# Weight conversion shared with GpSimd, a copy in halves, and a new order in the first turn of a gated linear attention + SSM kernel

## The chip, the cores and the metric

The kernel runs on one core of a Trainium2 chip. The metric is device time in microseconds (us), the median of several runs. All arithmetic is in float32, except the handling of the weights' bits. The engines are TensorE (PE, with its weight loads PEld), VectorE (DVE), ScalarE (ACT), GpSimd (POOL) and SyncE (SP, which here only issues DMAs).

## The reference

Two blocks follow each other: a gated linear recurrence over 4 batches x 8 heads x 768 steps with head dimension 48, and a gated state space block with model width 384 and inner width 512. `w_in`, `A_log` and `w_out` come as float64.

```python
for t in range(S):
    state = alpha[:, :, t, :, None] * state + np.einsum('bhd,bhe->bhde', k[:, :, t], v[:, :, t])
    y[:, :, t] = np.einsum('bhd,bhde->bhe', q[:, :, t], state)
x = y.transpose(0, 2, 1, 3).reshape(B, S, H * D)
proj = x @ w_in
val, gate = (proj[..., :D_inner], proj[..., D_inner:])
a = np.exp(A_log)[None, None, :]
for t in range(S):
    h = a[0, 0] * h + val[:, t, :]
    ys[:, t, :] = h
silu = gate * (1.0 / (1.0 + np.exp(-gate)))
out = silu * ys @ w_out
```

## The kernel before

The 4 x 768 steps are cut into 12 groups of 256 steps. A group `m` is prepared (attention inputs), then attended, then projected and written out; in turn `n` the projection and output of group `n` run beside the attention of group `m = n + 1` and the preparation of group `n + 2`. There is no scheduler: each engine runs its instructions in the order in which the source issues them, and the tile framework only adds the waits that data and buffers need.

**Preparation.** `alpha`, `q` and `k` arrive with time on the partitions. Groups 0 to 2 are turned by PE against an identity matrix: `turned` (L663) issues 16 matmuls (each runs as two passes, so the profile counts 32) into a pair of PSUM banks, and ACT copies the pair into SBUF: `alphas` (L677) for alpha, `straighten` (L681) for q and k. Later groups are turned by DVE (`products`, L643). Then DVE makes two running products along time, `P` (`scan_P`, L616) and `V` (`scan_V`, L625), and scales k by V and q by P (`scaled_k`, L600, into `Zk`; `scaled_q`, L593, into `Zq`).

**Attention of a group.** `first` multiplies `Zk` with `Zq` on PE (`scores`, L695) and masks the result (`masks`, L708: DVE one half, ACT a copy of the other, POOL its mask, L722). `second` forms half of the values and the states (`values`, `states`), which ACT copies into `dS` and POOL adds up (`add_up`, L785). `third` adds what the sums carry (`carried`), the other half of the values, and brings the result into the layout of the projection, `xT` (`join`, L843), by ACT copies and small DMAs ("moves"). In turn 0 half of the moves are issued by POOL, half by SP. Group 0 has shorter functions of its own (`first_values`, `first_states`, `first_carried`, `first_join`).

**Projection and output.** `project(n, cc)` (L858) handles a quarter of the inner width: six matmuls write the value half and the gate half of the PSUM tile `pvg`; DVE scans the first half into `hh`, ACT takes the silu of the second into `sg`; the returned function makes POOL multiply them into `f`. `output(n)` (L877) multiplies the four quarters of `f` by `w_out`. Its tile `pair` has two banks, one for each 128 steps: the first three quarters for both, then the last quarter for both, then ACT copies the two halves to `o_sb` and SP sends them off.

**Weights.** [...] `low(i)` (L531) is an ACT copy that scales the low words into an int32 tile `wr` (two buffers); `convert(i)` (L537) is a DVE shift (L544), a DVE OR (L546) and an int32 add of `wr` (L548, which the profile shows as `CUSTOM_DVE_ANT_0`). 128 x 768 words a piece. Projection `cc` needs piece `cc`, output pieces 4 and 5.

**Start.** `wide` holds v of group 0 with zeros between the heads, so that one matmul can cover a window; `wide_S` likewise for the first states. POOL clears all of `wide` (L892) and then issues the loads of v into it, builds the identity (`make_identity`), fills the ends of the raw tiles (L510), and copies the identity into `Zq` (L514). DVE clears `ends` and the rest in `constants` (L490). `keep_warm` (L686) issues three matmuls on zeros ahead of the first real work, from `ends`.

**Order of turn 0 before** (calls in the source; each puts its instructions at the end of their engines' queues):

```python
f0 = project(n, 0); low(2); tq = straighten(1, "q"); f0(); V = scan_V(1, P)
f1 = project(n, 1); low(3); scaled_k(1, tk, V); scaled_q(1, tq, P); alphas(2)
tk = straighten(2, "k"); convert(2); first(m); low(4); tq = straighten(2, "q"); f1()
convert(3); f2 = project(n, 2); second(m); low(5); f2(); convert(4)
f3 = project(n, 3); third(m); f3(); convert(5); P = scan_P(2); V = scan_V(2, P)
scaled_k(2, tk, V); scaled_q(2, tq, P)
```

(`load_...` and `junk` calls are left out here; `junk` is an ACT check of alpha that nothing waits for.)

Of the kernel before, what the change touches and what calls it, by code (L numbers as in the profile page):

```python
# [9 lines left out]
FP32 = mybir.dt.float32  # L10
# [3 lines left out]
ALU = mybir.AluOpType  # L14
# [331 lines left out]
def fast(  # L346
# [64 lines left out]
    def steps_of(name, m):  # L411
        return raws[name][:, ds(m % 2 * (2 * ROW + 16), 2 * ROW + 16)]
# [14 lines left out]
    def load_v(m, engine):  # L427
        if m >= N:
            return
        b, g = divmod(m, NG)  # L430
        for c in range(G):
            if m:
                to = vs[m % NV][:, c, :, 0:D]
            else:
                to = wide[:, c].rearrange("p (h d) -> p h d", d=D)[:, ::2, :]
            engine.dma_start(out=to, in_=v[b, :, ds(g * GC + c * C, C), :].rearrange("h p d -> p h d"))
# [51 lines left out]
    flag = const.tile([1, 1], I32, name="flag")  # L488

    def constants():  # L490
        nc.vector.memset(ends, 0.0)
        for al in als:
            nc.vector.memset(al[:, ::GP], 0.0)
        nc.vector.memset(minus, -1.0)
        nc.vector.memset(one, 1.0)
        nc.vector.memset(lower, FLOOR)
        for t in wide_S:
            nc.vector.memset(t, 0.0)
        nc.scalar.activation(spare, minus, AF.Exp)
        for t in vs:  # L500
            nc.vector.memset(t[:, :, :, D:64], 0.0)
        for t in dS[0] + dS[1]:
            nc.vector.memset(t[:, :, :, D:64], 0.0)
        for t in sums:
            nc.vector.memset(t[:, :, D:64], 0.0)
        nc.vector.memset(K0[:, :, :, D:], 0.0)
        make_identity(nc, ident)
        for name in "aqk":
            for m in range(2):
                nc.gpsimd.memset(steps_of(name, m)[:, 2 * ROW:], 1.0)  # L510
        for n, t in enumerate(Zqs):
            for i in range(2):
                rows = ds(64 * i, 64)
                nc.gpsimd.tensor_copy(out=t[rows, :, :, 0:D].rearrange("p u h d -> p (u h) d"),  # L514
                                      in_=ident[rows, None, ds(64 * i, D)].to_broadcast([64, 8 * G, D]))
            if n == 0:
                nc.gpsimd.memset(tri, 1.0)
                nc.gpsimd.affine_select(out=tri, in_=tri, compare_op=ALU.is_ge, fill=0.0, base=0,
                                        channel_multiplier=-1, pattern=[[1, C]])
                for h in range(2):  # L520
                    nc.gpsimd.tensor_copy(out=mask[ds(L * h, L)], in_=tri[ds(L * h, L), ds(L * h, L)])
# [15 lines left out]
    def convert(i):  # L537
        if i not in lows:
            low(i)
        bits, w = bits_of(i)  # L540
        hi = bits[:, :, :, 1]
        t = w.bitcast(U32)
        r = lows.pop(i)
        nc.vector.tensor_scalar(out=t, in0=hi, scalar1=3, scalar2=0x3FFFFFFF,  # L544
                                op0=ALU.logical_shift_left, op1=ALU.bitwise_and)
        nc.vector.scalar_tensor_tensor(out=t, in0=hi, scalar=0xC0000000, in1=t,  # L546
                                       op0=ALU.bitwise_and, op1=ALU.bitwise_or)
        nc.vector.tensor_tensor(out=w.bitcast(I32), in0=w.bitcast(I32), in1=r, op=ALU.add)  # L548

    def check_w(i):  # L550
        hi = bits_of(i)[0][:, :, :, 1].bitcast(FP32)
# [27 lines left out]
    def by_place(t):  # L579
        return t[:, 0:4 * GP].rearrange("p (h t) -> p h t", h=4)  # L580

    def by_runs(t):
        return t.rearrange("p h (c j) -> p h c j", j=NJ)
# [76 lines left out]
        yield  # L660


    def turned(m, name, t):  # L663
        raw = steps_of(name, m)
        tp = t.rearrange("p b x -> p (b x)").rearrange("p (j x) -> p j x", j=NJ)
        for j in range(NJ):
            for i in range(2):
                nc.tensor.matmul(tp[ds(64 * i, 64), j], raw[:, ds(i * ROW + j * D, 64)], ident,  # L668
                                 start=True, stop=True, skip_group_check=True)
        return tp.rearrange("p j (c h) -> p h c j", h=4)  # L670

    def bank_pair(tag=None):
        if tag:
            return ps_at.tile([C, 2, 512], FP32, tag=tag, name=tag)
        return ps_mm.tile([C, 2, 512], FP32, tag="mm", name="mm")

    def alphas(m, tag=None):  # L677
        nc.scalar.activation(by_runs(by_place(als[m % 2])[:, :, 1:GP]),  # L678
                             turned(m, "a", bank_pair(tag)), AF.Copy)

    def straighten(m, name, tag=None):  # L681
        t = plain(name)
# [3 lines left out]
    def keep_warm(n, w, tag="y"):  # L686
        t = bank_pair(tag)[:, 0]
        for _ in range(n):
            nc.tensor.matmul(t[:, 0:w], ends.rearrange("p h t -> p (h t)")[:, 0:C], ends.rearrange("p h t -> p (h t)")[:, 0:w], start=True, stop=True, skip_group_check=True)


    NS = S // L
# [184 lines left out]
    def output(n):  # L877
        b, g = divmod(n, NG)
        pair = ps_mm.tile([C, 2, 512], FP32, tag="mm", name="o")
        os = [pair[:, c, 0:DM] for c in range(G)]  # L880
        for ccs in (range(NI - 1), range(NI - 1, NI)):
            for c in range(G):
                for cc in ccs:
                    nc.tensor.matmul(os[c], fs[n][:, cc, ds(c * C, C)], w_outs[cc // 2][:, cc % 2, :],  # L884
                                     start=(cc == 0), stop=(cc == NI - 1))
        for c in range(G):
            o_sb = p2.tile([C, DM], FP32, tag="o_sb", name="o_sb")
            nc.scalar.activation(o_sb, os[c], AF.Copy)  # L888
            nc.sync.dma_start(out=out[b, ds(g * GC + c * C, C), :], in_=o_sb)


    nc.gpsimd.memset(wide, 0.0)  # L892
    both = [nc.sync, nc.scalar]
    load_steps("a", 0, both)
    load_steps("q", 0, both)
    load_steps("k", 0, both)
    load_steps("a", 1, [nc.sync])
    load_v(0, nc.gpsimd)
    for name in "kq":
        load_steps(name, 1, [nc.sync])  # L900
    nc.scalar.dma_start(out=a_log, in_=moe_A_log.rearrange("(a p) -> p a", p=C))
# [9 lines left out]
            next(steps, None)  # L911

    keep_warm(3, 256)
    alphas(0, "s")
    tq = straighten(0, "q")
    tk = straighten(0, "k")
    load_steps("a", 2, [nc.sync])
# [12 lines left out]
    tk = straighten(1, "k")  # L930
    scores(0)
    masks(0, True)
    P = scan_P(1)
    first_values(True)
    first_states(states(0))
    low(0)
    convert(0)
    first_carried((1,))
    first_values(False)
    first_carried((2, 3))  # L940
    first_join()
    for half in range(2):
        load_w_out(half, nc.sync)
    load_v(2, nc.sync)
    low(1)
    convert(1)
    junk(0)

    def first(m):
# [18 lines left out]
    for n in range(N):  # L968
        m = n + 1
        if n == 0:  # L970
            f0 = project(n, 0)
            low(2)
            tq = straighten(1, "q")
            f0()
            V = scan_V(1, P)
            f1 = project(n, 1)
            low(3)
            scaled_k(1, tk, V)
            scaled_q(1, tq, P)
            alphas(2)  # L980
            load_raw("a", 3, nc.sync)
            tk = straighten(2, "k")
            load_raw("k", 3, nc.sync)
            convert(2)
            first(m)
            low(4)
            tq = straighten(2, "q")
            f1()
            convert(3)
            f2 = project(n, 2)  # L990
            second(m)
            low(5)
            f2()
            convert(4)
            f3 = project(n, 3)
            third(m)
            load_v(3, nc.sync)
            load_raw("q", 3, nc.sync)
            f3()
            convert(5)  # L1000
            junk(1)
            P = scan_P(2)
            V = scan_V(2, P)
            scaled_k(2, tk, V)
            scaled_q(2, tq, P)
            junk(2)
        else:
            first(m)
            if n > 1:
                load_raw("q", n + 2, nc.sync)  # L1010
            go(1)
            f0 = project(n, 0)
            second(m)
            f0()
            load_raw("a", n + 3, nc.sync)
            go(2)
            f1 = project(n, 1)
            f1()
            if n == N - 2:
                for i in range(0, 2):  # L1020
                    check_w(i)
            third(m)
            load_v(m + 2, nc.sync)
            load_raw("k", n + 3, nc.sync)
            go(1)
            f2 = project(n, 2)
            f2()
            if n == N - 2:
                check_w(2)
            if n == N - 1:  # L1030
                check_flag()
            go(1)
            f3 = project(n, 3)
            f3()
            go(2)
        if n == N - 2:
            for i in range(3, NW):
                check_w(i)
            check_end()
        if n == N - 1:  # L1040
            value = nc.values_load(flag[0:1, 0:1], min_val=0, max_val=1)
        output(n)
# [39 lines left out]
```

## Time and profile before

| | us |
|---|---|
| median of 3 runs (lowest to highest) | 293.84 (293.11 to 293.91) |
| profiled execution | 296.36 |
| its span (first to last instruction) | 294.6 |
| PE busy | 278.6 (95%) |
| DVE busy | 215.3 (73%) |
| POOL busy | 112.0 (38%) |
| ACT busy | 108.0 (37%) |
| mean granted PE clock | 0.982 |
| start of the first projection (group 0, quarter 0) | 25.38 |
| start of turn 1 (scores of group 2) | 59.10 |

The profile is of one execution, with some us of its own. Instructions are named by engine, line, output and inputs. The "chain of waits" follows back from the last instruction to what released it; in order of time it shows which engine led when. The timeline lists instructions with start and duration, and in brackets how long the engine was idle before and what ended that. The table by stretches of time gives each engine's busy time (and instruction count), then the granted clock of PE (1.00 is full), the DMA share and GB/s. A line of waits names who waited, for whom, the total, the number of times and the longest. An engine that is off the chain costs nothing by being idle.

### The profile page before, as it was taken

To read this page: it belongs to the slowest core of one execution; us is meant where nothing else is said; L and a number is where in the kernel's file an instruction comes from. 1 tells how busy PE (TensorE), PEld (TensorE's weight loads), DVE (VectorE), ACT (ScalarE), POOL (GpSimd) and SP (SyncE) were. 2 spreads that over 40 slices of the span, in tenths; PEclk is the share of its full clock that TensorE was granted. 3 is DMA by queue.
4 is the path that set the end of the run, shared out by engine and by line. 5 is a ranking of instruction groups with operands and counts; after the bars stand their busy time and mean duration, and the time that the engine had idled before them with its cause. 6 is when DMAs were issued, how large, how long until landed. Compare 5 with 4: busy or idle time off the path is not lost.

```text
span 294.6 us, 9484 instructions
## 1 busy us (share of the span) xinstructions
PE 278.6 (95%) x4064; PEld 220.8 (75%) x4064; DVE 215.3 (73%) x254; ACT 108.0 (37%) x235; POOL 112.0 (38%) x126
## 2 busy tenths in 40 slices
PE   7979999599999999999999999999999999999990
PEld 5967886288778788688688688787787786886860
DVE  6798888939859768689597697697698697269320
ACT  2565556323335244144135235325333351421111
POOL 8300346315416417237146056155155173141110
PEclk9999999959999999999999999999999999999997
DMA  6999580813396494693691891981973911100101
GB/s 203 351 265 365 136 174 17 194 57 89 74 246 141 108 260 92 155 233 65 152 271 41 179 242 51 226 185 47 253 154 86 248 30 32 57 17 25 56 6 61
DMA packets 51812, 41.57 MB, mean 141 GB/s; under 512 B 27344, under 2 KB 49552, under 8 KB 51760
## 3 DMA queue, kind: packets, MB, share of 16 engines
q1 hardware_dynamic: 50544, 39.72, 52.6%
q8 instruction: 34, 0.56, 0.8%
q10 hardware_dynamic: 960, 0.59, 0.8%
q0 software_dynamic: 256, 0.56, 0.6%
q14 instruction: 18, 0.15, 0.2%
HBM read 32.88 MB, written 4.72 MB: 128 GB/s over the span
## 4 chain that ended last, share of the span: by engine, by line
PE 86%; DVE 8%; issue 1%; ACT 1%; POOL 1%; DVEq 0%; POOLq 0%
PE pvg L866 45%; PE o L884 19%; PE y L738 4%; PE s L765 4%; PE y L751 4%; PE s L704 3%; PE mm L704 3%; DVE P L621 2%; DVE V L638 2%; DVE Zk L605 1%; DVE Zq L596 1%; PE s L668 1%; PE y L813 1%; PE y L805 1%; PE mm L668 1%
## 5 line engine op out<-in xcount | busy, mean ns | idle before, releaser
L866 PE MATMUL pvg<-xT,w_in 128*128 128x256 f32 x576 | 135.6, 389 | 0.6 <-ACT xT L827 0.6
L866 PEld LDWEIGHTS pvg<-xT,w_in 128*128 128x128 f32 x576 | 107.6, 192 | 18.1 <-ACT xT L827 0.7
L875 POOL TENSOR_TENSOR f<-sg,hh 128x256 f32<-128x256 f32 x48 | 57.2, 1193 | 68.4 <-ACT sg L874 68.4
L884 PE MATMUL o<-w_out,f 128*128 128x384 f32 x192 | 64.5, 487 | 1.1 <-DVE w_out L548 0.7
L874 ACT ACTIVATE sg<-pvg 128x256 f32<-128x256 f32 x48 | 18.4, 384 | 101.4 <-DVE hh L869 72.6
L884 PEld LDWEIGHTS o<-w_out,f 128*128 128x128 f32 x192 | 36.2, 190 | 24.6 <-issue 1.3
L869 DVE TENSOR_TENSOR_SCAN hh<-a_dec,hh,pvg 128x256 f32<-128x256 f32 x32 | 23.5, 733 | 25.8 <-PE pvg L866 25.0
L722 POOL TENSOR_TENSOR AK<-AK,mask 128x512 f32<-128x512 f32 x11 | 14.6, 1328 | 69.8 <-ACT AK L720 69.8
L785 POOL TENSOR_TENSOR sum<-sum,dS 128x192 f32<-128x192 f32 x37 | 27.4, 739 | 24.1 <-ACT dS L773 22.4
L621 DVE TENSOR_TENSOR_SCAN P<-al,lower 128x1028 f32<-128x1028 f32 x12 | 27.8, 2313 | 3.6 <-ACT al L678 3.4
L638 DVE TENSOR_TENSOR_SCAN V<-al,ends 128x1028 f32<-128x1028 f32 x12 | 27.9, 2322 | 0.1
L888 ACT ACTIVATE o_sb<-o 128x384 f32<-128x384 f32 x24 | 10.5, 488 | 45.4 <-PE o L884 41.5
L719 DVE TENSOR_TENSOR A<-s,mask 128x256 f32<-128x256 f32 x11 | 4.7, 424 | 21.2 <-PE s L704 21.2
L586 DVE STREAM_TRANSPOSE al<-raw_a 128x1024 f32<-128x1024 f32 x9 | 18.4, 2045 | 0.0
L586 DVE STREAM_TRANSPOSE k<-raw_k 128x1024 f32<-128x1024 f32 x9 | 18.4, 2042 | 0.0
L586 DVE STREAM_TRANSPOSE q<-raw_q 128x1024 f32<-128x1024 f32 x9 | 18.2, 2019 | 0.0
L704 PEld LDWEIGHTS s<-Zq,Zk 48*64 48x64 f32 x384 | 10.1, 140 | 9.9 <-issue 9.9
L869 DVE TENSOR_TENSOR_SCAN hh<-a_dec,pvg 128x256 f32<-128x256 f32 x16 | 10.8, 675 | 9.1 <-PE pvg L866 9.1
L704 PE MATMUL s<-Zq,Zk 48*64 48x112 f32 x384 | 12.7, 273 | 4.0 <-DVE Zq L596 4.0
L751 PEld LDWEIGHTS y<-Zq,sum 48*64 48x64 f32 x656 | 12.0, 134 | 4.5 <-POOL sum L785 2.7
L751 PE MATMUL y<-Zq,sum 48*64 48x64 f32 x656 | 14.7, 222 | 0.6 <-issue 0.6
L596 DVE TENSOR_TENSOR Zq<-q,P 128x1024 f32<-128x1024 f32 (+1 forms) x13 | 14.8, 1141 | 0.3
(121 smaller groups left out, 344.3 us busy)
## 6 DMA issues: line engine op xcount, KB each, us to landing
out_dram<-o_sb SPq DMA_DIRECT2D x24, 192.0 KB, 3.6
v<-in_v_dram SPq DMA_DIRECT2D x22, 192.0 KB, 3.7
raw_a<-in_alpha_dram SPq DMA_DIRECT2D x18, 184.0 KB, 4.8
raw_k<-in_k_dram SPq DMA_DIRECT2D x18, 184.0 KB, 4.4
raw_q<-in_q_dram SPq DMA_DIRECT2D x18, 184.0 KB, 4.0
raw_a<-in_alpha_dram SPq DMA_DIRECT2D x18, 176.0 KB, 5.1
raw_k<-in_k_dram SPq DMA_DIRECT2D x18, 176.0 KB, 4.4
raw_q<-in_q_dram SPq DMA_DIRECT2D x18, 176.0 KB, 4.2
```

Source lines behind the costliest of these rows:

```text
L586: nc.vector.transpose(out=by_runs(to).rearrange("p h c j -> p h j c"), in_=raws[name][:, 0:4 * ROW].rearrange("p (h j d) -> p h j d", h=4, ...
L596: nc.vector.tensor_mul(Zqs[m % 2][:, ds(u0, n), :, D:].rearrange("p u h t -> p h u t"), t[:, :, at].rearrange("p h (u t) -> p h u t", t=L) ...
L621: nc.vector.tensor_tensor_scan(out=P, data0=al[:, 0:4 * GP], data1=lower.rearrange("p h t -> p (h t)"), initial=0.0, op0=ALU.mult, op1=ALU ...
L638: nc.vector.tensor_tensor_scan(out=V[:, ::-1], data0=al[:, 1:4 * GP + 1][:, ::-1], data1=ends.rearrange("p h t -> p (h t)")[:, ::-1], init ...
L704: nc.tensor.matmul(scs[m][c][ds(L * h, L), i, ds(p * (L + D), L + D)], Zk[rows, c, p, ds(h * L, L)], Zq[rows, u, p], start=True, stop=True ...
L751: nc.tensor.matmul(ys[m][ds(64 * s, 64), i, e, ds(u * L, L)], Ss[j][rows, p, :], Zqs[m % 2][rows, u, p, D:], start=False, stop=True, skip_ ...
L785: nc.gpsimd.tensor_add(Ss[j][:, :, 0:D], Ss[j - 1][:, :, 0:D], part)
L866: nc.tensor.matmul(pj, w_ins[cc][:, kk, vg, :], xT[:, kk, :], start=(kk == 0), stop=(kk == NK - 1))
L869: nc.vector.tensor_tensor_scan(out=hh, data0=a_dec[:, cc:cc + 1].to_broadcast([C, GC]), data1=pv, initial=prev_h[cc][:, GC - 1:GC] if n % ...
L874: nc.scalar.activation(sg, pg, AF.Silu)
L875: return lambda: nc.gpsimd.tensor_mul(fs[n][:, cc, :], sg, hh)
L884: nc.tensor.matmul(os[c], fs[n][:, cc, ds(c * C, C)], w_outs[cc // 2][:, cc % 2, :], start=(cc == 0), stop=(cc == NI - 1))
```

## The change

1. **Start.** The identity is built first on POOL, then its copies into the first `Zq`, and only then are the loads of v issued. The ends of the raw tiles and the zeros of `wide` are set by DVE, of `wide` and `wide_S[1:]` the gaps alone. `wide_S[0]` is cleared first, and `keep_warm` reads it.
2. **First alpha.** PE turns the first half, ACT copies it, PE turns the second half, ACT copies it.
3. **Weights.** The int32 add of `convert` is issued on POOL.
4. **Before turn 0.** `convert(0)` and `convert(1)` come earlier, the scan P of group 1 after them; q of group 1 is straightened and its scan V made before turn 0.
5. **Turn 0.** Each `f` product follows its projection directly; conversions 3 and 4 and P of group 2 come before projection 2, conversion 5 before projection 3, V of group 2 and the last product `f3` before the attention's third part with its moves.
6. **Output.** In every turn the copy and the DMA of the first half are issued after its last matmul, ahead of the last matmul of the second half.

```diff
     def constants():
-        nc.vector.memset(ends, 0.0)
+        make_identity(nc, ident)
+        nc.vector.memset(wide_S[0], 0.0)
+        for name in "aqk":
+            for m in range(2):
+                nc.vector.memset(steps_of(name, m)[:, 2 * ROW:], 1.0)
+        for c in range(G):
+            nc.vector.memset(wide[:, c].rearrange("p (h d) -> p h d", d=D)[:, 1::2, :], 0.0)
...
+        nc.vector.memset(ends, 0.0)
+        for t in wide_S[1:]:
+            nc.vector.memset(t.rearrange("p (h d) -> p h d", d=D)[:, 1::2, :], 0.0)
...
             if n == 0:
+                load_v(0, nc.gpsimd)
                 nc.gpsimd.memset(tri, 1.0)
...
-        nc.vector.tensor_tensor(out=w.bitcast(I32), in0=w.bitcast(I32), in1=r, op=ALU.add)
+        nc.gpsimd.tensor_tensor(out=w.bitcast(I32), in0=w.bitcast(I32), in1=r, op=ALU.add)
...
-    def alphas(m, tag=None):
-        nc.scalar.activation(by_runs(by_place(als[m % 2])[:, :, 1:GP]),
-                             turned(m, "a", bank_pair(tag)), AF.Copy)
+    def alphas(m, tag=None, parts=1):
+        t = bank_pair(tag)
+        to = by_runs(by_place(als[m % 2])[:, :, 1:GP])
+        for n in range(parts):
+            js = range(NJ // parts * n, NJ // parts * (n + 1))
+            tp = turned(m, "a", t, js)
+            nc.scalar.activation(to[:, :, :, js.start:js.stop], tp[:, :, :, js.start:js.stop], AF.Copy)
...
-            nc.tensor.matmul(t[:, 0:w], ends.rearrange("p h t -> p (h t)")[:, 0:C], ends.rearrange("p h t -> p (h t)")[:, 0:w], start=True, stop=True, skip_group_check=True)
+            nc.tensor.matmul(t[:, 0:w], wide_S[0][:, 0:C], wide_S[0][:, 0:w], start=True, stop=True,
+                             skip_group_check=True)
...
+        def evict(c):
+            o_sb = p2.tile([C, DM], FP32, tag="o_sb", name="o_sb")
+            nc.scalar.activation(o_sb, os[c], AF.Copy)
+            nc.sync.dma_start(out=out[b, ds(g * GC + c * C, C), :], in_=o_sb)
+
         for ccs in (range(NI - 1), range(NI - 1, NI)):
             for c in range(G):
                 for cc in ccs:
                     nc.tensor.matmul(os[c], fs[n][:, cc, ds(c * C, C)], w_outs[cc // 2][:, cc % 2, :],
                                      start=(cc == 0), stop=(cc == NI - 1))
-        for c in range(G):
-            o_sb = p2.tile([C, DM], FP32, tag="o_sb", name="o_sb")
-            nc.scalar.activation(o_sb, os[c], AF.Copy)
-            nc.sync.dma_start(out=out[b, ds(g * GC + c * C, C), :], in_=o_sb)
...
+                if ccs.stop == NI:
+                    evict(c)
...
-    nc.gpsimd.memset(wide, 0.0)
...
-    load_v(0, nc.gpsimd)
...
-    alphas(0, "s")
+    alphas(0, "s", 2)
...
-    P = scan_P(1)
+    low(0)
+    convert(0)
     first_values(True)
     first_states(states(0))
-    low(0)
-    convert(0)
+    low(1)
+    convert(1)
+    P = scan_P(1)
     first_carried((1,))
     first_values(False)
     first_carried((2, 3))
     first_join()
+    tq = straighten(1, "q")
+    V = scan_V(1, P)
...
-    low(1)
-    convert(1)
```

The order of turn 0 after the change, written as above:

```python
f0 = project(n, 0); low(2); scaled_k(1, tk, V); f0(); f1 = project(n, 1)
scaled_q(1, tq, P); alphas(2); f1(); tk = straighten(2, "k"); convert(2); low(3); first(m)
convert(3); tq = straighten(2, "q"); low(4); convert(4); P = scan_P(2)
f2 = project(n, 2); f2(); second(m); low(5); convert(5)
f3 = project(n, 3); f3(); V = scan_V(2, P); third(m)
scaled_k(2, tk, V); scaled_q(2, tq, P)
```

More of the change, by code (lines that the diff above doesn't have):

```diff
@@ L496, in constants @@
         nc.vector.memset(lower, FLOOR)
-        for t in wide_S:
-            nc.vector.memset(t, 0.0)
+        nc.vector.memset(ends, 0.0)
+        for t in wide_S[1:]:
+            nc.vector.memset(t.rearrange("p (h d) -> p h d", d=D)[:, 1::2, :], 0.0)
         nc.scalar.activation(spare, minus, AF.Exp)
@@ L506, in constants @@
         nc.vector.memset(K0[:, :, :, D:], 0.0)
[L507 to L510, printed above, removed]
         for n, t in enumerate(Zqs):
@@ L660, in products, with turned @@
         yield
-    def turned(m, name, t):
+    def turned(m, name, t, js=range(NJ)):
         raw = steps_of(name, m)
         tp = t.rearrange("p b x -> p (b x)").rearrange("p (j x) -> p j x", j=NJ)
-        for j in range(NJ):
+        for j in js:
             for i in range(2):
@@ L972, in fast @@
             low(2)
-            tq = straighten(1, "q")
+            scaled_k(1, tk, V)
             f0()
-            V = scan_V(1, P)
             f1 = project(n, 1)
-            low(3)
-            scaled_k(1, tk, V)
             scaled_q(1, tq, P)
@@ L981, in fast @@
             load_raw("a", 3, nc.sync)
+            f1()
             tk = straighten(2, "k")
@@ L984, in fast @@
             convert(2)
+            low(3)
             first(m)
+            convert(3)
+            tq = straighten(2, "q")
             low(4)
-            tq = straighten(2, "q")
-            f1()
-            convert(3)
+            convert(4)
+            P = scan_P(2)
             f2 = project(n, 2)
+            f2()
             second(m)
             low(5)
-            f2()
-            convert(4)
+            convert(5)
             f3 = project(n, 3)
+            f3()
+            V = scan_V(2, P)
             third(m)
@@ L998, in fast @@
             load_raw("q", 3, nc.sync)
-            f3()
-            convert(5)
             junk(1)
-            P = scan_P(2)
-            V = scan_V(2, P)
             scaled_k(2, tk, V)
```

## The prediction

> **What bounds the kernel now.** I read the page first: TensorE (PE) is busy 95% of the span, so whatever shortens or lengthens the time does so by opening or closing gaps in PE. The chain of waits, in order of time, shows where the gaps are. From 66.8 us to the end it is PE back to back, some 21 us a turn. Ahead of that VectorE (DVE) leads, above all here:
>
> ```profile
> 50.15 0.96 DVE w_out L548
> 51.11 2.22 DVE P L621
> ...
> 53.99 2.58 DVE V L638
> ...
> 56.59 1.23 DVE Zk L605
> 57.81 1.15 DVE Zq L596
> ...
> 59.10 1.77 PE s L704 x32
> 60.87 1.49 PE mm L704 x32
> 62.36 4.41 PE pvg L866 x12
> ```
>
> PE has finished the first output at 56.01 and waits 3.09 us for the scaled q of group 2. Its next pieces are slow: in the later turns the same three take 0.93, 0.77 and 2.79 us, here 3.18 more. The table by stretches shows why (PE busy, then the other engines, then the granted clock):
>
> ```profile
> 56.00:58.00 2.00, 0.01 (x1) 0.00 (x0) 1.97 (x3) 0.87 (x2) 0.00 (x0) 1.00 1.09 245
> 60.00:61.00 1.00, 1.00 (x29) 1.00 (x25) 0.08 (x1) 0.00 (x0) 0.00 (x0) 0.50 0.04 14
> 66.00:67.00 1.00, 1.00 (x23) 0.64 (x24) 0.19 (x1) 0.00 (x0) 0.00 (x0) 1.00 0.94 289
> ```
>
> After the gap the clock is 0.50 until about 65.4. So the edge of turn 0 costs 3.1 us of waiting and 3.2 us of slow clock, and the change aims there. Two more readings decide what it can get. The timeline of DVE and GpSimd (POOL):
>
> ```profile
> 72.57 2.30 DVE L638 TENSOR_TENSOR_SCAN V<-al,ends 128x1028 f32<-128x1028 f32 x1
> 72.96 2.43 POOL L875 TENSOR_TENSOR f<-sg,hh 128x256 f32<-128x256 f32 x1 [0.59 <-ACT sg L874]
> 79.37 0.73 POOL L875 TENSOR_TENSOR f<-sg,hh 128x256 f32<-128x256 f32 x1 [1.44 <-ACT sg L874]
> 86.03 1.29 POOL L722 TENSOR_TENSOR AK<-AK,mask 128x512 f32<-128x512 f32 x1 [5.94 <-ACT AK L720]
> 39.92 1.83 POOL L722 TENSOR_TENSOR AK<-AK,mask 128x512 f32<-128x512 f32 x1 [7.70 <-ACT AK L720]
> 40.76 1.81 DVE L548 CUSTOM_DVE_ANT_0 w_in<-w_in,wr 128x1536 uint16<-128x1536 uint16 x1
> ```
>
> A POOL product that takes 0.73 alone takes 2.43 beside a DVE scan and ends 0.5 after it; a DVE add that takes 0.96 alone takes 1.81 beside a POOL product. So a POOL operation and a DVE operation with two SBUF operands do not overlap; they take turns. The shift L544 is held too (0.86 at 48.17 beside a product, 0.55 alone). Then the waits and the end of the chain:
>
> ```profile
> ACT sg L874 <- DVE hh L869: 72.6, 38, 3.5
> DVE hh L869 <- PE pvg L866: 34.2, 37, 3.6
> 282.55 5.17 PE o L884 x16
> 287.72 0.02 issue
> 287.74 0.06 ACT o_sb L888
> ```
>
> ScalarE's (ACT) silu reads the second half of `pvg`, the scan hh the first; silu waits for hh each time, and hh waits for the matmuls of both halves. The first half of `o` is complete a column-half's two passes (0.65) before 287.72, yet its copy starts after all 16. So accesses to one PSUM tile by different engines are ordered by the whole tile, whichever half they touch.
>
> **The change part by part.** The profiled execution took 296.36 (span 294.6 and 1.76 around it); the median of the timed runs is 293.84. I work out differences within the span and apply them to the median.
>
> *Start: 0.0, between -0.7 and +0.3.* The warm-up matmuls now wait for a memset of 336 columns (a third of 1.05) instead of 1028 (0.92) and start about 0.55 earlier. The first alpha transposes can follow at 4.5 instead of 5.01, since raw_a lands at 0.81 + 3.6 = 4.4 and the identity comes first on POOL. The copy in halves would save half of its 1.02. But by the rule by tile the second 16 passes wait for the first copy. First half: 16 slow passes at 0.107 and a drain end at 6.5. Copy: 0.57 (the 448-column copy L720 takes 0.55), 7.1. Second half: 9.3 if the clock is still low, copy 9.9, against 9.33 before; with a clock that rises at 7.4 as before, 9.0. Back comes the stretch of the first scan P (2.64 against 2.29 elsewhere), which POOL's copies of the identity at 8.14 caused; these are now earlier. Sum 0.55 - 0.35 = +0.2 to -0.7; I take 0. load_v(0) moves behind those copies: issue ends about 5.1, landing 6.4 later at 11.5, and the first reader is at 18.1, so it costs nothing with 6 us of cover. The narrower memsets lie on DVE before 5.9, where it idles until 9.35.
>
> *Until scores(1).* P(1) was hidden at 19.09-21.38 (the sums L822 waited for ACT until 21.53 anyway). Straightening q of group 1 fills PE's 0.56 wait before the first projection. DVE saves two adds of 0.96 and V(1) comes earlier; PE reaches scores(1) at 36.2 instead of 36.63. This only moves the start of what follows.
>
> *Low bits on POOL: the main term.* The trace has no integer add on POOL. Its products give 0.60 for 192 columns, 0.73 for 256, 1.27 for 512: 0.19 plus 2.1 ns a column, 1.81 for 768. Bounds: DVE's own 0.96, and 2.6 for an integer operation that is slower than a product. I take 1.81. The Trainium skill (GPSIMD Engine Reference, section 3.1) gives 4497 ns for an add of 2048 columns, by proportion an estimate of 1.69, and advises against moving elementwise work there; by it the sum would be 0.4 lower. Its 2.2 ns a column stands beside the products' 2.1 here; no run shows the add itself.
>
> From the masks of group 1 (38.3) to the scaled q of group 2, DVE has to take turns with POOL for: three conversions of 0.55 + 0.96, P 2.29, V 2.30, Zk and Zq 2.3, ratio 0.1 = 11.5. POOL brings a mask product 1.27, three adds 5.4, f2 and f3 1.46, three sums 1.86 = 10.0. That is 21.5 in turns, less some 0.15 hidden at each change-over. Before, it was 14.4 (three adds more on DVE) and 5.9, together 20.3. The adds leave DVE, but the turn-taking grows by 1.2. Laid out in program order with these durations, a change-over at each: mask product until 40.8, add 3 until 42.9, add 4 waits behind conversion 4 and P until 47.7, f2 48.6, sums 50.0 to 51.4, add 5 behind conversion 5 and V until 55.2, f3 56.8. hh2 now stands behind P(2) on DVE, silu and the evictions of dS behind it on ACT, so the sums start late: PE is through with projection 3 at 46.9 and gets the first sum at 50.0, a gap of 3.1 that was not there. Output then waits for add 5 (53.6 to 55.4) and ends at 59.8 with the stall below; scores(2) starts at 59.8. The same layout of the program before gives 58.8 (59.10 measured). So turn 0 ends **1.0 later**. With adds of 1.3 it ends 0.5 earlier, with 2.6 it ends 5.3 later. f3 ahead of the moves lets it end before the last quarter of output; POOL's moves issue until 58.9, land 1.9 later at 60.8, and projection (1,0) needs them at 61.5: covered by 0.7.
>
> *Clock: -1.6, between -3.2 and 0.* A gap of 3.1 again, about as long as the one that halved the clock. If it does so again, the slow stretch (6.3 after PE resumed) would run from 50.1 to 56.4; it doubles 2.9 of work until 53.6, of which the wait for add 5 hides 1.8, and adds 0.5 after it: 1.6 instead of 3.2. If later gaps hold it low, the full 3.2 is back; if it never falls, all is saved.
>
> *Output's eviction between the halves: 10 x 0.78 + 0.4 = +8.2.* The copy of half 0 is now issued before the last quarter's matmuls of half 1, which write the same tile. By the rule by tile they wait for it. The pass ends 0.49 after its start where the next would start after 0.32 (0.16 lost), ACT starts 0.02 later, copies 0.49, and PE follows ACT after 0.05 to 0.13 (21.50 to 21.55, 25.25 to 25.38): 0.72 to 0.80 a turn, 0.78 taken. Behind it on PE stand the next turn's scores, and nothing in turns 1 to 11 is waiting for anything but PE. Turn 0's is in the layout; the last turn gets back the 0.39 of the second copy. Bounds: 0 if halves are independent (then -0.4 at the end alone), 9.
>
> Sum: 0 + 1.0 - 1.6 + 8.2 = +7.6: **301.4**.
>
> **Rivals.** (a) *Halves are independent*: the matmuls of half 1 do not wait. No stall, the start gains 1.3 (0.5 + 0.45 + 0.35), scores(2) 0.9 earlier, the end 0.4, the clock 1.6: 290.9, between 289.2 and 292.5. For it speaks only that the halves are two separate column ranges; against it that silu waits for hh 38 times. It decides as soon as the price per turn is below about 0.1. The Trainium skill (PSUM — Partial Sum Buffer, section "PSUM bank collisions raise a hardware error") has accesses to different banks run side by side, so the chip would allow it; the trace shows this program not using that. Chance 0.13. (b) *POOL's integer add takes 2.6 or more*: 4.3 more in turn 0, 305 to 307. Nothing in the trace shows integers there. 0.10. (c) *The clock never falls*: 299.8, since the gap may be shorter than laid out; 0.3, inside the forecast's range. Forecast with (c): 0.74; 0.03 for the rest.
>
> **The numbers.** Forecast's own range: 297.5 (adds of 1.3, full clock, the better start) to 304 (full clock loss, adds of 2.1). With most of (b) the range is 297.0 to 306.5; it leaves out (a) and a tail, 0.18. A measurement here tells 0.3% (0.9 us) from no change. Faster by more: 0.12, nearly all of (a); within: 0.03; slower: 0.85.
>
> **What would show it.** A PE gap of 0.6 to 0.8 before the last quarter of each `o`, ended by ACT o_sb; a gap of about 0.7 inside the first alpha; POOL adds near 1.8 alone and over 3 beside P and V; a PE gap near 47 ended by POOL's sum; scores(2) at 59 to 61. If the copies of `o` start inside the output and PE does not pause, the forecast is wrong by its largest term; if scores(2) starts before 57, the layout by turns is wrong.

## The result and the profile after

The changed kernel takes 306.5 us (median of 4 runs, 305.01 to 308.83) against 293.88 for the kernel before (293.11 to 294.95): 1.0434 times as long, 95% interval 1.035 to 1.0518. The direction of the forecast was right. The time is 5.1 us above its 301.4, at the very top of its range. The profiled execution is the one of 305.01, with a span of 303.3 us. Ratios here and below are of undisturbed executions, medians of all; on one chip, where single executions of the kernel before went from 292.67 to 301.23, the two can differ by some tenths of a per cent.

PE is busy 279.9 us, as before (278.6), in a span that is 8.7 us longer: the loss is gaps. The chain of waits of the changed kernel (start, duration, what) in turn 0:

```profile
24.32 0.91 PE mm L672 x13
25.23 2.28 issue
27.51 1.31 PE mm L672 x19
...
50.30 1.31 POOL sum L794
51.61 0.07 issue
51.68 0.60 POOL sum L794
...
52.36 2.47 POOL sum L794
...
54.87 0.70 PE y L760 x16
55.57 6.90 PE o L898 x14
...
63.95 0.93 PE s L713 x32
64.88 0.77 PE mm L713 x32
65.65 2.79 PE pvg L875 x12
```

The first three lines are new and were not foreseen: the straightening of q of group 1, now ahead of the first projection, stops after 13 of its 32 passes for 2.28 us in which PE waits for nothing that the profile shows. Later PE waits for POOL's sums until 54.87, and most of the output then runs at half clock (6.90 us for 14 passes that take 4.53 elsewhere). Scores(2) start at 63.95 instead of 59.10, but they and the projection behind them run at full pace now. That projection ends at 68.44, against 66.77 before: 1.7 us of the 8.7. The other 7.0 come behind it.

The table by stretches (PE busy, then the other engines, then the granted clock) shows where the clock was low this time:

```profile
54.00:56.00 2.00, 1.13 (x17) 1.01 (x18) 1.90 (x3) 0.36 (x1) 2.00 (x2) 0.50 0.00 0
60.00:62.00 2.00, 2.00 (x8) 1.14 (x6) 0.00 (x0) 0.00 (x0) 1.88 (x4) 1.00 0.96 200
```

It fell at 53.1 and rose at 59.9, as long as before (6.83 us) but 5.7 us earlier. In the timeline of POOL and DVE the integer add takes 1.84 us alone and 3.67 beside the scan of P:

```profile
38.13 1.84 POOL L552 TENSOR_TENSOR w_in<-w_in,wr 128x768 int32<-128x768 int32 x1 [1.50 <-DVE w_in L550]
45.45 2.29 DVE L625 TENSOR_TENSOR_SCAN P<-al,lower 128x1028 f32<-128x1028 f32 x1
45.67 3.67 POOL L552 TENSOR_TENSOR w_out<-w_out,wr 128x768 int32<-128x768 int32 x1 [0.96 <-DVE w_out L550]
49.79 1.37 DVE L550 SCALAR_TENSOR_TENSOR w_out<-wobits,w_out 128x768 uint32<-128x768 uint32 x1
50.30 4.51 POOL L794 TENSOR_TENSOR sum<-sum,dS 128x192 f32<-128x192 f32 x3
52.06 2.38 DVE L642 TENSOR_TENSOR_SCAN V<-al,ends 128x1028 f32<-128x1028 f32 x1
```

The three sums, which took 2.54 together in the old order, start at 50.30 and take 4.51: by the chain above the first takes 1.31 beside DVE's OR, the second 0.60, and the third 2.47 beside V. PE's waits and the end of the chain:

```profile
PE o L898 <- ACT o_sb L892: 7.0, 12, 0.6
PE y L760 <- POOL sum L794: 4.9, 2, 3.1
PE mm L672 <- issue: 2.3, 1, 2.3
```

```profile
291.91 4.53 PE o L898 x14
296.46 0.50 ACT o_sb L892
297.01 0.93 PE o L898 x2
```

In each of 12 turns the output's last two passes wait for the copy of the other half. The pitch of a turn (start of one output to the next) is 21.76 us in most turns, from 20.91: 0.85 a turn.

### The profile page after: what moved, and what is told of

Same layout as the page of the kernel before. It is cut to its first block, busy times and chain, and to the rows that moved or that the text cites. A ratio compares the mean times of both kernels' runs of the same rounds, so it can differ in the third digit from the quotient of the medians.

```text
span 303.3 us, 9489 instructions
## 1 busy us (share of the span) xinstructions
PE 279.9 (92%) x4064; PEld 218.2 (72%) x4064; DVE 216.3 (71%) x256; ACT 109.3 (36%) x236; POOL 127.3 (42%) x125
## 4 chain that ended last, share of the span: by engine, by line
PE 89%; ACT 3%; DVE 3%; issue 2%; POOL 1%; DVEq 0%; POOLq 0%; ACTq 0%
PE pvg L875 43%; PE o L898 22%; PE y L747 4%; PE y L760 4%; PE s L774 4%; PE s L713 3%; PE mm L713 3%; PE mm L672 3%; ACT o_sb L892 2%; POOL sum L794 1%; PE y L697 1%; PE s L672 1%; DVE P L625 1%; PE y L822 1%; DVE V L642 1%
## 5 line engine op out<-in xcount | busy, mean ns | idle before, releaser
L875 PE MATMUL pvg<-xT,w_in 128*128 128x256 f32 x576 | 133.6, 385 | 0.0
L898 PE MATMUL o<-w_out,f 128*128 128x384 f32 x192 | 69.4, 506 | 7.0 <-ACT o_sb L892 7.0
L794 POOL TENSOR_TENSOR sum<-sum,dS 128x192 f32<-128x192 f32 x37 | 28.7, 775 | 19.9 <-ACT dS L782 18.1
L892 ACT ACTIVATE o_sb<-o 128x384 f32<-128x384 f32 x24 | 11.8, 490 | 50.3 <-PE o L898 50.3
L600 DVE TENSOR_TENSOR Zq<-q,P 128x1024 f32<-128x1024 f32 (+1 forms) x13 | 16.4, 1264 | 0.3
L552 POOL TENSOR_TENSOR w_in<-w_in,wr 128x768 int32<-128x768 int32 x4 | 9.4, 2360 | 15.5 <-ACT wide_S L829 12.4
L609 DVE TENSOR_TENSOR Zk<-k,V 128x1024 f32<-128x1024 f32 (+1 forms) x13 | 14.7, 1134 | 0.2
```

Of the source, the lines that this page charges most:

```text
L794: nc.gpsimd.tensor_add(Ss[j][:, :, 0:D], Ss[j - 1][:, :, 0:D], part)
L875: nc.tensor.matmul(pj, w_ins[cc][:, kk, vg, :], xT[:, kk, :], start=(kk == 0), stop=(kk == NK - 1))
```

## The experiments

Times are medians; the ratio is to the kernel before in the same comparison, with its 95% interval.

| kernel | us | ratio |
|---|---|---|
| changed kernel | 306.5 | 1.0434 (1.035 to 1.0518) |
| e1 output as before | 298.15 | 1.0117 (1.0066 to 1.0169) |
| e2 output's halves in two tiles | 297.09 | 1.0107 (1.0064 to 1.0149) |
| e3 before, interleaved copies | 302.44 | 1.0245 (1.0191 to 1.0299) |
| e4 before, new start | 294.19 | 0.9966 (0.9931 to 1.0002) |
| e5 e2, adds on DVE | 296.75 | 1.0066 (1.0033 to 1.0098) |
| e6 before, adds on POOL | 299.81 | 1.0173 (1.0135 to 1.0211) |
| e7 e2, straightening behind the projection | 295.13 | 1.0000 (0.9968 to 1.0032) |
| e8 e2, P(2) behind h3 | 298.38 | 1.0048 (0.9999 to 1.0096) |
| e9 before, straightening ahead | 298.12 | 1.0067 (1.0021 to 1.0112) |
| e10 e7, adds on DVE | 292.80 | 0.9909 (0.9871 to 0.9948) |
| e11 before, new start, two tiles | 295.65 | 0.9981 (0.9936 to 1.0025) |
| e13 e11, 12 warm passes | 294.64 | 1.0006 (0.9969 to 1.0043) |
| e14 e10, P(2) behind h2 | 293.65 | 0.9952 (0.9912 to 0.9991) |
| e15 e10, P(2) behind h3 | 294.84 | 0.9961 (0.9922 to 1.0000) |
| e17 e11, 6 warm passes | 291.24 | 0.9890 (0.9845 to 0.9935) |
| e18 e10, 4 warm passes | 291.42 | 0.9881 (0.9835 to 0.9927) |

### The output's copies: e1, e2, e3

e1 takes the output's code of before into the changed kernel; e3 takes the new one into the kernel before. e2 keeps the interleaved copies and changes one line of the changed kernel:

```
-        os = [pair[:, c, 0:DM] for c in range(G)]
+        os = [pair[:, 0, 0:DM], bank_pair("y")[:, 0, 0:DM]]
```

> The changed kernel with the output's code of before: all 16 passes, then the two copies. Theory 1 (the copy of the first half and the passes into the second wait for each other in every turn): the turn's pitch falls from 21.76 back to 20.91 us, 0.85 us in each of 11 turns less about 0.4 us that the last turn's early copy had won, so 306.5 - 9.0 = 297.5 us. Rival (the longer turns come from elsewhere, say from ScalarE's other order): the pitch stays near 21.76 and the time stays at 305 to 308 us. What is then left over the time of before, about 3.6 us, would be turn 0.

> The changed kernel with the interleaved copies kept, but the output's second half in another PSUM tile (the one named y, which is free by then). Theory 1a (the wait follows the tile, as the order of PSUM accesses is kept for whole tiles): PE runs 16 passes without a stop, the pitch is 20.9 us and the time is that of the kernel with the output as before less 0.3 to 0.8 us, about 297.0 us. Rival 1b (ScalarE's reading of PSUM holds PE's writing whichever tile): PE still stops for about 0.58 us a turn, 305 to 308 us.

> The kernel before with nothing changed but the interleaved copies of the output, in one tile. Theory 1: 11 turns of 0.85 us less 0.4 us: 293.9 + 9.0 = 302.9 us (302.1 to 303.4), a PE group for the output of 69 to 70 us with 7 us idle ahead. Rival: the wait costs only in the changed kernel, where turn 0 has left ScalarE late: no change, 293.9 us.

e1 and e2 fell by 8.4 and 9.4 us, as theory 1 and 1a had it; the pitch in e2 is 20.93. In e2's chain of waits the passes of both halves follow each other without a stop, though ACT copies the first half under the last two:

```profile
101.40 1.94 PE y L898 x6
103.33 0.65 PE o L898 x2
103.98 0.65 PE y L898 x2
104.62 0.93 PE s L713 x32
```

```profile
104.01 0.49 ACT L892 ACTIVATE o_sb<-o 128x384 f32<-128x384 f32 x1 [3.22 <-PE o L898]
```

So it is the shared tile that makes PE wait, not ACT's reading beside PE's writing. e3 shows the price without anything else: +8.0 us in the medians (1.9 to 3.0% by the ratio), pitch 21.76, and the same 7.0 us of waiting for o_sb.

### The start: e4

e4 is the kernel before with the new `constants()`, `turned`, `alphas(0, "s", 2)`, `keep_warm` and the place of `load_v(0)`.

> The kernel before with only the changed start: constants on VectorE in another order, the load of v(0) later on GpSimd, alpha of the first group copied in halves. Theory (the scan of P starts 0.76 us sooner and everything behind it follows): 293.9 - 0.76 = 293.1 us. Rival 1 (halves gain nothing, as the scan waits for the second copy, which waits for PE): 293.9 us. Rival 2 (PE's early pace costs later: the 2.28 us in which PE waits for nothing shown stands at the same time of day, near 25 us, and now falls into a gap): 294 to 296 us.

The profile has P at 9.05 (8.59 in the changed kernel, 9.35 before). The ratio's interval, -2.0 to +0.1 us, holds the theory's -0.76; it leans to a gain of about 1 us and speaks against rival 2. Rival 1, no gain, lies just inside it and is not excluded.

### The adds: e5, e6, and e10 against e7

```
-        nc.gpsimd.tensor_tensor(out=w.bitcast(I32), in0=w.bitcast(I32), in1=r, op=ALU.add)
+        nc.vector.tensor_tensor(out=w.bitcast(I32), in0=w.bitcast(I32), in1=r, op=ALU.add)
```

This in e2 is e5, and in e7 (below) e10; the reverse in the kernel before is e6.

> The changed kernel with the output's second half in another PSUM tile (so PE doesn't wait there), and the low bits added by VectorE again, in the changed order. Theory 2 (GpSimd's six adds of 1.8 to 3.7 us hold the sums of turn 0 and let VectorE wait for its turn): scores(2) starts about 1.7 us sooner, 297.1 - 1.7 = 295.4 us, and the clock may lose a window less. Rival 2a (the order of turn 0, above all P(2) ahead of the third h and the straightening ahead of the projection, is what costs): 296.8 to 297.5 us.

> The kernel before with nothing changed but the engine of the add of the low bits, now GpSimd. Theory 2: the adds alone make turn 0 longer by 1 to 2.5 us, 295.5 to 297 us. Rival 2a (the adds are hidden in the old order, where VectorE is the late one and wins some 0.9 us each for them): 293.5 to 294.5 us.

> As e7 (second tile, straightening behind the projection), and the low bits added by VectorE again: the changed order alone. Theory 2: 0.5 to 1.7 us less than e7, 0.994 to 0.998 of the time before. Rival 2a (the order alone sets turn 0, the adds are neutral in it): the same as e7, 1.000 of the time before.

e5 gained about 0.4% (1.2 us) on e2, less than the 1.7 expected and within the intervals. e10 gained 0.9% (2.7 us) on e7, and the intervals do not overlap. In e6 the adds alone cost 5.1 us: both numbers on record were too low. Its timeline of POOL, and PE's longest wait, show why:

```profile
51.34 2.11 POOL L850 DMA_DIRECT2D xT<-yst  x4
55.45 3.79 POOL L548 TENSOR_TENSOR w_out<-w_out,wr 128x768 int32<-128x768 int32 x1
```

```profile
PE o L884 <- POOL w_out L548: 7.6, 2, 6.3
```

In the old order the last add stands on POOL behind the moves, a sum and f3, starts at 55.45 and then takes turns with DVE's V and Zk, and the output waits for it; after that wait the clock is halved from 57.9 to 64.7. In the order of the change POOL's adds cost 1.2 (e5) to 2.7 us (e10) by the middles instead of 5.1. The order doesn't make them a gain.

### The straightening ahead of the projection: e7, e9

e7 is e2 with this; e9 moves the same two lines ahead, in the kernel before.

```
     first_join()
-    tq = straighten(1, "q")
-    V = scan_V(1, P)
...
             low(2)
+            tq = straighten(1, "q")
+            V = scan_V(1, P)
             scaled_k(1, tk, V)
```

> The changed kernel with the output's second half in another PSUM tile, and q of group 1 straightened (and V(1) scanned) behind the first projection of turn 0 again. Theory 3 (the 2.28 us in which PE waits for nothing shown, in the midst of 32 short passes, come from instructions that arrive late: short passes use them up faster than the long passes of a projection): the gap is gone, since the long passes now stand there; the first projection starts near 25.4 instead of 28.8 us and turn 0 ends up to 1.5 us sooner, 295.6 to 297 us. Rival 3a (the gap belongs to the straightening, wherever it stands, by its tile or its input): the gap moves along behind the projection, and the time stays at 297 us.

> The kernel before with only this moved: q of group 1 is straightened, and V(1) scanned, ahead of the first projection of turn 0 instead of behind it. Theory 3 (short passes use up PE's instructions faster than they are fetched): a gap of 2.3 to 3 us stands inside the 32 short passes near 25 us, the first projection starts near 29 instead of 25.4 us, and the time is 1 to 3 us longer than before. Rival 3b (the gap in the changed kernel came with the other changes, e.g. the shifted loads of w_out; the step alone costs nothing, since the projection's xT can be copied meanwhile): no gap, within 0.5 us of before.

e7 gained 1.07% (3.2 us) on e2, and the intervals do not overlap: by the middles the largest loss in turn 0. The times show it, not e7's profiled execution (297.21 against 297.25 for e2's), in which the clock was halved from 21.9 to 25.3 and scores(1) started as late as in the changed kernel (37.88). e9 lost 0.2 to 1.1% (0.6 to 3.3 us), with the same stop after the same 13 passes, if shorter. Its chain of waits:

```profile
24.82 0.91 PE mm L668 x13
25.73 1.06 issue
26.79 1.32 PE mm L668 x19
```

What ends the stop is in the trace's DMA records. A queue that carries nothing but instructions (34 packets, 0.56 MB in the page of the changed kernel) moves blocks of 16 KB, which start 3 to 19 us apart. The block of that time lands at 26.08 in the changed kernel and PE goes on at 27.51, 1.43 later; in e1, e2, e5, e8 and e9 it goes on 1.48, 1.41, 1.44, 1.61 and 1.39 us after the landing, while the stop itself is anything from 1.06 to 3.25 long.

The place of the stop settles what it is. In all six traces it stands behind the same number of PE's instructions: 961 on record, weight loads and waits included. In e3 and e6, where other passes stand at that place, PE stops behind 961 as well, for 0.33 and 0.58, and goes on 1.59 and 1.61 after the landing (26.71 and 27.81). The other place with such stops is behind 705, 256 instructions earlier: 0.59 in e14, 0.86 in e7, 2.03 in e17, each until 1.42 to 1.46 after a block has landed. So PE runs out of instructions at the end of a block, whatever stands there, and how long it stops depends on how soon it gets there. In the kernel before the block starts at 25.13 and lands at 26.10, but PE is busy with the long passes of the projection until 28.4, and there is no stop. Why the block comes so late (it starts between 24.1 and 26.9 in all of these) was not settled; the DMA engines are full at that time (share 1.02 from 24 to 28 us).

The Trainium skill (Runtime: NRT & Kernel Launch, section "Instruction fetch mechanics") has instructions refilled in blocks of 16 KiB, 256 instructions, at a cost that is mostly hidden. The block size and the 256 instructions between the two places agree; here the refill is exposed by 1 to 3 us. That passes of 59 to 70 ns use instructions up faster than the projection's of 230 fits e7 and e9.

### The place of P(2): e8, e14, e15

```
-            P = scan_P(2)
             f2 = project(n, 2)
...
             f3 = project(n, 3)
+            P = scan_P(2)
             f3()
```

This is made in e2 (e8) and in e10 (e15); e14 puts P(2) between `project(n, 2)` and `f2()` in e10.

> The changed kernel with the output's second half in another PSUM tile, and the scan of P(2) (2.3 us on VectorE) moved from ahead of the third projection's h to behind the fourth's. Theory 2b (P(2) delays h, sg and with them ScalarE's copy of the parts of the state, which GpSimd's sums wait for): the parts are copied 2 us sooner, the third sum ends near 53 instead of 54.8 us, and scores(2) starts 1.0 to 1.6 us sooner: 295.5 to 296.1 us. Rival (the sums wait for GpSimd's adds and the port, not for their parts): 296.8 to 297.5 us.

> As e10 (the changed order with q straightened behind the projection, the adds on VectorE, the second tile), and the scan of P(2) moved behind the third projection's h. Theory 2b (P(2)'s 2.2 us ahead of h is what makes the sums and the rows behind them late): h, sg and f of the third projection come 2.2 us sooner, but P(2) then stands beside the sums and may hold GpSimd for part of it; output of turn 0 ends 0.3 to 1.5 us sooner, 0.985 to 0.990 of the time before. Rival (the end of turn 0 is set by the last conversion and the last f, which all stand behind P(2) on VectorE in either order): the same as e10, 0.991.

> As e10, and the scan of P(2) moved behind the fourth projection's h, as in e8, but without the gap and the lost clock that covered it there. Theory 2b: the third sum ends near 47 instead of 49 us and the output of turn 0 ends 0.7 to 2.2 us sooner, 0.983 to 0.989 of the time before. Rival 1 (as in e8's profile, P(2) now holds the last sum and f): the same as e10, 0.991. Rival 2 (V(2), Zk(2) and Zq(2) come too late for scores(2)): slower than e10 by 0.5 us or more.

e8 settles nothing: its ratio is 0.6% below e2's, the intervals overlap, and in its profiled execution the stop was 3.25 us long and the clock was halved from 26.3 to 33.2. e14 and e15 are not faster than e10; their intervals overlap with its, and their middles are 0.4 and 0.5% above. In e15's profile the third sum takes 2.65 us beside P(2), where it takes 0.6 alone, and ends at 51.2, against 49.06 in e10: rival 1. P(2) holds somebody at each place tried. Theory 2b fell.

### The lost clock: e11, e13, e17, e18

e11 is e4 with the output of e2. e13 and e17 add, with 12 and with 6 passes:

```
         output(n)
+        if n == 0:
+            keep_warm(6, 256, "s")
```

e18 adds `keep_warm(4, 192, "s")` ahead of `third(m)` in turn 0 of e10.

> The kernel before with the new start and the interleaved copies with the second half in another tile; turn 0 and the adds as before. If the parts add up: start -0.3 to -0.8 us, the earlier copy of the last turn -0.3 to -0.8 us: 0.994 to 0.998 of the time before. If one of them only moves a wait: 1.000.

> As e11, with 12 passes of 256 columns that compute nothing behind the output of turn 0, where PE otherwise waits 3.1 us for VectorE. Theory 4 (the granted clock falls because PE stood idle there, and the passes behind it then run at half pace for one or two stretches of 3.41 us): no stretch at half clock near 60 us, scores(2) and the projection behind it take 1.0 to 2.0 us less, 0.5 to 1.5 us less than e11. Rival 4a (the clock falls whatever PE does there, or the time is not set by PE there): the same as e11 or 0.2 us more.

> As e13, but with 6 passes of 256 columns that compute nothing instead of 12. In e13 the 12 passes took 5.19 us (0.43 each, not the 0.22 reckoned with) and held scores(2) back by about 1 us; six take 2.6 us of the 3.1 us in which PE waits. Theory 4 (the gap costs by the clock that it takes away): the clock holds as in e13 and scores(2) starts as in e11, so 1 us less than e13 and 0.5 to 1.5 us less than e11: 0.993 to 0.997 of the time before. Rival 4a (the clock there is not worth anything, as VectorE sets the pace behind it): the same as e11, 0.998 to 1.001.

> As e10, with 4 passes of 192 columns that compute nothing ahead of the carried part of group 1, where PE waits 3.46 us for GpSimd's sum; they can start only when ScalarE has copied the states out of their tile (47.7 us), and then fill 1.3 us of the gap. Theory 4: the clock falls in fewer executions, 0.5 to 1 us less than e10: 0.987 to 0.990 of the time before. Rival 4b (PE has by then stood idle for 2 us, and the clock falls all the same): the same as e10, 0.991.

e11 kept little: -0.2%, no difference within its interval. In e13's chain of waits the filling was twice as long as I had reckoned (a call is two instructions, x24), and scores(2) start at 59.99 instead of 59.29 (e11):

```profile
54.75 5.19 PE s L697 x24
59.95 0.04 issue
59.99 1.00 PE s L713 x32
```

Its clock held in every execution (mean 0.993 to 0.998, where e11 had 0.973 to 0.998), and the time stayed. That the delay took what the clock gave is likely, but not shown. With half the passes, e17 is 0.9% (2.7 us) below e11 and 1.1% below the kernel before; six of its seven executions had a clock of 0.992 to 0.999 and took 290.2 to 293.0. Its profiled execution is the seventh, with the stop of 2.03 us described above and the clock halved from 24.0 to 34.3, so that the gain is shown by the times and not by a timeline. e17 also lies 3.4 us below e13, more than the delay of 0.7 that e13's trace shows: the cause of the rest is not shown. In e18 the clock held in all six executions (0.990 to 1.000, in e10 0.977 to 0.992), but its time against e10 is -0.3%, inside the intervals. e17 and e18 are the fastest of all, by their ratios 3.2 and 3.5 us below the kernel before.

## Why the prediction missed by 5 us

The profiled executions differ by 8.65 us (305.01 less 296.36), 1.05 more than the 7.6 of the sum. The rest of the miss lies in what the differences were applied to: the profiled execution before is 2.5 above its median, the one after 1.5 below its own. Within the spans two errors partly cancel. Up to the end of the projection behind scores(2) the terms said -0.6 (0 + 1.0 - 1.6), and the traces show +1.7; behind it they said 8.2, and the traces show 7.0. So the steps that failed are those of turn 0: the straightening that was to fill a wait, and the clock.

**Start (0.0).** It was the better end of its bounds: P 0.76 us sooner. The halves do wait for each other, as said: PE stands 0.7 us for ACT between them; but the clock rose at 5.3 us (7.6 before), so the second half took 1.14. In e4, with the same code and the clock up at 6.3, P was 0.30 sooner.

**Until scores(1) (36.2).** This step failed. Scores(1) started at 37.84. "Straightening q of group 1 fills PE's 0.56 wait" counted its passes and not their instructions. It was put at nothing and cost 3.2 us by e7, the stop and the clock together: PE stops for 2.28 us at the end of a block of instructions. With it behind the projection they start at 35.52 (e10) and 36.28 (e14), as laid out; in e7's own trace, with its halved clock, at 37.88.

**Low bits on POOL (1.81 each; turn 0 +1.0).** The price was right: 1.81 to 1.84 alone, no dearer for integers. So rival (b), whose 305 to 307 hold the time, is not what happened. Taking turns was right too (3.67 beside P, sums late, and the PE gap of 3.1 that was laid out: 48.55 to 51.66). The layout came out late because it began 1.6 late and let the three sums pass at 1.4 together, while DVE's OR and V came between them: the last ended at 54.8 where 51.4 was laid out, and a second PE gap of 1.8 stood ahead of it. Scores(2) started at 63.95, outside the 59 to 61 given as a sign. By the runs the adds cost 2.7, and the rest of the order gains some 2.1 (e10's -2.7 less e11's -0.6): +0.6, near the +1.0, but each of these is uncertain by 1 to 2 us.

**Clock (-1.6).** This step failed. The slow stretch was as long as before (6.83 us). PE worked in it for 5.06 us, against 6.52 before; as an estimate, half of that is lost, 2.5 against 3.3, so that 0.7 was saved between the profiled executions and not 1.6. And the credit was taken against a profiled execution (296.36) and applied to a median (293.84) whose executions had probably lost less (their clocks are not on record). In one later comparison, executions of the kernel before at a mean clock of 0.982 to 0.985 took 294.55 to 296.71, at 0.987 to 0.989 293.12 to 294.80. The sum should have said what part of the profiled execution's own stretch the median doesn't have.

**Output's eviction (+8.2).** Right in place, cause and nearly in size. Measured are 0.85 a turn, not 0.78: besides the copy (0.56 with its hand-overs) the two groups take 4.53 + 0.91, against 5.17 in one piece, 0.27 lost where 0.16 was laid out. Behind turn 0 the traces still show only 7.0 in all, since two turns of the profiled execution before took 21.56 and 21.24 instead of 20.91. In the kernel before it costs 8.0 (e3), in the changed one 8.4 to 9.4 (e1, e2). The Trainium skill's rule (PSUM — Partial Sum Buffer, section "PSUM bank collisions raise a hardware error") that accesses to different banks run side by side is what e2 shows: ACT copies one bank from 104.01 to 104.50 while PE writes another, and PE doesn't wait. In the changed kernel the halves lie in two banks as well and PE waits all the same, so the order is that of the program's tiles. Rival (a) was right about the chip and wrong about the program, as the prediction put it.

Taken along the chain of kernels: order, start and tail -2.7 (e10), adds +2.7 (e10 to e7), straightening +3.2 (e7 to e2), one tile for both halves +9.4 (e2 to the changed kernel), together +12.6. These are successive differences, so they add up to the whole by construction; each carries 1 to 3 us of uncertainty, and the split depends on the order in which the parts are taken (the adds cost 1.2 from e5 to e2).

## What to carry to other kernels

When copies are moved in between matmuls, look at the unit by which accesses are ordered: halves of one tile serialise, two tiles run free, and 0.85 us a turn hangs on one line. When work is moved to fill a wait of PE, count instructions as well as time, and when a term rests on the clock, ask how much of it the executions behind the median lost. An engine with time to spare (POOL at 38%) is not free if its operations take turns with the engine that leads.

## What the runs showed of the hardware

The granted clock changes in steps: the traces' stretches at half clock last 3.41, 6.83 or 10.24 us, multiples of 3.413. The stretch of 3.41 just ahead of a fall held PE work of 0 (e6), 0.57 us (e10), 0.63 (before), 1.40 (changed kernel) and as much as 1.96 (e4) and 2.11 (e7), so PE need not have been idle for the whole of one. With 1.56 (e4) and 1.70 (changed kernel, 25.79 to 29.21) the clock held. In these traces it fell in each such stretch with less than 1.56 and in none with more than 2.11; in between both occur. In the kernel before PE was busy for 3.10 us of the first slow stretch of 3.41 and the clock rose only after the second; in e10 it was busy for 3.39, and one was enough.

The Trainium skill (TensorE: Matmul & The Clock Gate, section "What's actually happening") names a free-running window of 3413 ns, which agrees, and a fall after at least one idle window; the traces have it fall after windows that were up to 62% busy.

Between 20 us and the last output, the profiled executions here lost none (e14), one (e10), two (before), three (e1) or four (e8) of these stretches. The clock's first rise comes at anything from 4.7 (e5) to 10.7 us (e11), so where in the window an execution begins varies, and much of the spread between executions of one kernel goes with it: of 120 later ones of the kernel before, those with a mean clock up to 0.985 have a median of 296.1 us, those from 0.986 to 0.989 294.2, and those over 0.993 293.3.
